# Transposing the first blocks of each memory layer on TensorE instead of by DMA, with a scheduling order of their own

**Chip, cores, metric.** One core of one Trainium2 chip. The metric is the device time of one execution in microseconds (us).

## The reference

Four blocks on a 2048x512 residual stream: memory layer, linear attention, the same memory layer again, linear attention again. Only the memory layer matters here:

```python
def _A_ref(x, mem0, Wq, Wk, Wv, Wo, seg_len):      # x 1x2048x512, 32 heads of 128, seg_len 32, M = 8
    ...
    mem = mem0
    for s in range(n_seg):                          # 64 steps, each needs the memory of the one before
        xs = x[:, s * seg_len:(s + 1) * seg_len, :].copy()
        h = jnp.concatenate([mem, xs], axis=1)      # 8 memory rows + 32 rows of x
        q = jnp.einsum('btd,dhe->bhte', h, Wq)      # k, v likewise
        ...                                         # masked softmax attention, o
        o = jnp.einsum('bhte,hed->btd', o, Wo)
        mem = o[:, :M, :].copy()
        outs.append(o[:, M:, :])
...
x = x + _A_ref(_layernorm(x, axis=-1), A_mem0, A_Wq, A_Wk, A_Wv, A_Wo, A_seg_len)
x = x + _B_ref(_layernorm(x, axis=-1), B_wqkv, B_wo)
x = x + _A_ref(...)                                 # and _B_ref(...) again
```

## The kernel before

The kernel builds a list of nodes (one to some dozens of instructions each) and orders them at build time: each node has a kind and a step, a table `OFFSET` gives the kind's offset, and the priority is step times 13.5 plus offset. An engine then takes the most urgent node that is ready. The waits follow from the data that nodes read and write.

A step projects a block of 32 rows: the 8 memory rows and 24 of the 32 of x. The other 8 rows of four steps are gathered in a "left-over" block, so there are five blocks (and five output projections) in four steps. Queries and keys come out of the projection with the tokens on the partitions and have to be transposed, through an SBUF image, by one of two ways:

```python
def turned(W, key, blk, bkeys, b, dst, dkey, urgent, dma):
    tl = project(W, key, blk, bkeys, b, urgent)                 # 16 matmuls 128x512 into one PSUM bank
    k = img_no[0] % NI if urgent else NI                        # image slot: 3 for the steps, ONE for left-over blocks
    img_no[0] += urgent
    nd = evac(img[:, k, :], lambda: tl.f32()[:, :], 512, ...)   # ScalarE or VectorE
    if dma:
        add("sp", lambda e: e.dma_start_transpose(dst..., img[:, k, :]), 1.25, reads=[("img", k)], ...)
        return nd
    tt = P.tile()
    def tr(pe):                                                 # 16 transposes and 16 weight loads
        for i in range(4):
            for j in range(4):
                r = pe.transpose(tt.bf16()[...], img[:, k, o:o + 32], id_sb[:, :], tile_position=(0, 32 * j))
        return r
    add("pe", tr, ...)
    evac(dst..., lambda: tt.bf16()[:, 0:512], 512, ...)         # a second copy, PSUM to SBUF
    return nd
```

In a step, half of the queries and keys (`b` = 0) goes by DMA and half over TensorE; a left-over block goes by DMA altogether. The loads of the output weights Wo stand in SyncE's order between the transposes:

```python
for i in range(4):                                              # Wo in four quarters of 1 MB
    nd = add("sp", lambda s, hs=hs: s.dma_start(Wo_sb[:, hs, :], wo_view[:, hs, :]), 0.9, writes=[("Wo", i)],
             dsem="dWo%d" % i, after=[late[-2]], ...)           # after the load before the last one
    late.append(nd)                                             # late = [Wq, Wk, Wv, Wo0, Wo1, Wo2, Wo3]
```

The softmax here doesn't subtract the row's maximum and nothing guards it: scores larger than these inputs give would overflow.

## Time and profile before

| | us |
|---|---|
| median of the 3 runs | 1868.53 |
| lowest, highest | 1867.57, 1869.97 |

From the page of the profile (the lines of windows, chain and SyncE that carry the prediction are shown there). First the span, the row of busy times, then two DMA queues with packets, MB and share:

```profile
span 1867.5 us, 95161 instructions
...
PE 1762.9 (94%) x43796; PEld 1201.8 (64%) x43905; DVE 1065.5 (57%) x3267; ACT 1160.3 (62%) x3015; POOL 74.5 (4%) x172
...
q1 hardware_dynamic: 220656, 62.58, 18.1%
...
q8 instruction: 343, 5.62, 1.3%
```

TensorE is busy 94% of the span. q1 carries the transposes.

### The profile page before, as it was taken

To read this page: it belongs to the slowest core of one execution; us is meant where nothing else is said; L and a number is where in the kernel's file an instruction comes from. 1 tells how busy PE (TensorE), PEld (TensorE's weight loads), DVE (VectorE), ACT (ScalarE), POOL (GpSimd) and SP (SyncE) were. 2 spreads that over 40 slices of the span, in tenths; PEclk is the share of its full clock that TensorE was granted. 3 is DMA by queue.
4 is the path that set the end of the run, shared out by engine and by line. 5 is a ranking of instruction groups with operands and counts; after the bars stand their busy time and mean duration, and the time that the engine had idled before them with its cause. 6 is when DMAs were issued, how large, how long until landed. Compare 5 with 4: busy or idle time off the path is not lost.

```text
span 1867.5 us, 95161 instructions
## 1 busy us (share of the span) xinstructions
PE 1762.9 (94%) x43796; PEld 1201.8 (64%) x43905; DVE 1065.5 (57%) x3267; ACT 1160.3 (62%) x3015; POOL 74.5 (4%) x172
## 2 busy tenths in 40 slices
PE   4899999999999999999799999999999999999996
PEld 1566767666666667676456666766667666676662
DVE  1455555656565565655445556556555665565555
ACT  2466666666666666666456666666666666666655
POOL 2000000000000000000000000000000000000000
PEclk8999999999999999999899999999999999999999
DMA  9512121221222121211021222122122221212213
GB/s 336 126 35 42 35 43 37 43 40 37 43 37 43 35 46 37 45 38 40 21 42 35 42 38 48 40 37 45 37 44 42 45 43 38 45 38 54 45 34 124
DMA packets 228256, 96.86 MB, mean 52 GB/s; under 512 B 211624, under 2 KB 222000, under 8 KB 226320
## 3 DMA queue, kind: packets, MB, share of 16 engines
q1 hardware_dynamic: 220656, 62.58, 18.1%
q0 software_dynamic: 5616, 15.60, 2.7%
q10 hardware_dynamic: 1584, 12.58, 1.7%
q8 instruction: 343, 5.62, 1.3%
q14 instruction: 57, 0.47, 0.1%
HBM read 29.89 MB, written 10.49 MB: 22 GB/s over the span
## 4 chain that ended last, share of the span: by engine, by line
PE 85%; DMA 10%; ACT 2%; DVE 2%; issue 1%; SPq 0%; ACTq 0%; DVEq 0%
PE pb L753 39%; PE pb L952 15%; DMA arena_sb<-arena_sb 8%; PE pb L928 4%; PE pb L837 3%; PE pb L775 3%; PE pb L993 3%; PE pb L1088 2%; PE pb L975 2%; PE pb L854 2%; PE pb L892 2%; PE pb L1124 1%; PE pb L868 1%; PE pb L1190 1%; PE pb L867 1%
## 5 line engine op out<-in xcount | busy, mean ns | idle before, releaser
L591 ACT ACTIVATE arena_sb<-pb 128x512 bf16<-128x512 f32 (+6 forms) x1309 | 682.0, 530 | 341.5 <-PE pb L753 272.5
L753 PE MATMUL pb<-Wk_sb,arena_sb 128*32 128x512 bf16 x5120 | 347.7, 383 | 5.5 <-DMA Wk_sb<-in_A_Wk_dram 5.5
L753 PE MATMUL pb<-Wv_sb,arena_sb 128*32 128x512 bf16 x5120 | 352.2, 381 | 0.0
L753 PE MATMUL pb<-Wq_sb,arena_sb 128*32 128x512 bf16 x5120 | 342.2, 383 | 5.4 <-DVE arena_sb L592 4.8
L952 PE MATMUL pb<-Wo_sb,arena_sb 128*32 128x256 bf16 x10368 | 312.3, 275 | 4.9 <-DMA Wo_sb<-in_A_Wo_dram 2.9
L592 DVE CAST arena_sb<-pb 128x128 bf16<-128x128 f32 (+3 forms) x452 | 179.9, 398 | 221.3 <-PE pb L975 110.0
L952 PEld LDWEIGHTS pb<-Wo_sb,arena_sb 128*32 128x32 bf16 x10368 | 274.2, 97 | 20.7 <-DMA Wo_sb<-in_A_Wo_dram 3.4
L913 DVE TENSOR_TENSOR arena_sb<-arena_sb 32x256 bf16<-32x256 bf16 x512 | 212.1, 414 | 50.9 <-ACT arena_sb L909 38.8
L592 DVE COPY arena_sb<-pb 128x512 bf16<-128x512 bf16 (+2 forms) x325 | 121.2, 380 | 191.6 <-PE pb L775 183.9
L753 PEld LDWEIGHTS pb<-Wk_sb,arena_sb 128*32 128x32 bf16 x5120 | 136.9, 97 | 133.6 <-DMA Wk_sb<-in_A_Wk_dram 5.6
L753 PEld LDWEIGHTS pb<-Wq_sb,arena_sb 128*32 128x32 bf16 x5120 | 124.2, 96 | 111.3 <-DVE arena_sb L592 10.6
L753 PEld LDWEIGHTS pb<-Wv_sb,arena_sb 128*32 128x32 bf16 x5120 | 132.5, 97 | 98.1 <-issue 2.8
L591 ACT ACTIVATE outW_sb<-pb 128x128 fp32r<-128x128 f32 x228 | 63.2, 277 | 200.0 <-PE pb L952 198.0
L775 PEld LDWEIGHTS pb<-id_sb,arena_sb 128*32 128x32 bf16 x4096 | 76.4, 96 | 95.0 <-ACT arena_sb L591 47.5
L775 PE MATMUL pb<-id_sb,arena_sb 128*32 128x128 bf16 x4096 | 103.1, 220 | 24.1 <-ACT arena_sb L591 20.2
L928 PE MATMUL pb<-arena_sb 128*128 128x128 bf16 x1024 | 118.7, 217 | 5.5 <-DVE arena_sb L915 5.5
L592 DVE CAST outW_sb<-pb 128x128 fp32r<-128x128 f32 x96 | 28.0, 292 | 161.6 <-ACT outW_sb L591 161.6
L915 DVE TENSOR_TENSOR arena_sb<-arena_sb 32x64 bf16<-32x64 bf16 x512 | 110.8, 216 | 15.7
L844 ACT ACTIVATE arena_sb<-pb 128x256 bf16<-128x256 f32 x252 | 92.1, 383 | 41.1 <-PE pb L837 33.1
L929 PE MATMUL pb<-arena_sb 128*128 128x32 bf16 x1024 | 109.7, 178 | 0.0
L928 PEld LDWEIGHTS pb<-arena_sb 128*128 128x128 bf16 x1024 | 87.8, 96 | 7.2 <-DVE arena_sb L915 5.9
L837 PE MATMUL pb<-arena_sb 128*128 128x32 bf16 x2016 | 89.3, 177 | 2.8 <-DMA arena_sb<-arena_sb 2.5
(109 smaller groups left out, 2270.2 us busy)
## 6 DMA issues: line engine op xcount, KB each, us to landing
arena_sb<-arena_sb SPq DMA_TRANSPOSE x384, 2.5
Wq_sb<-in_A_Wq_dram ACTq DMA_DIRECT2D x1, 4096.0 KB, 13.5
Wk_sb<-in_A_Wk_dram ACTq DMA_DIRECT2D x1, 4096.0 KB, 23.7
Wv_sb<-in_A_Wv_dram ACTq DMA_DIRECT2D x1, 4096.0 KB, 34.4
Wo_sb<-in_A_Wo_dram SPq DMA_DIRECT2D x4, 1024.0 KB, 7.5
xs_scratch<-x_sb POOLq DMA_DIRECT2D x32, 128.0 KB, 2.0
pq_scratch<-arena_sb POOLq DMA_DIRECT2D x32, 128.0 KB, 2.5
x_sb<-xs_scratch POOLq DMA_DIRECT2D x16, 128.0 KB, 2.3
```

The source lines that it names most:

```text
L591: return e.activation(o() if callable(o) else o, i() if callable(i) else i, ACTF.Copy)
L592: return e.tensor_copy(o() if callable(o) else o, i() if callable(i) else i)
L753: r = pe.matmul(tl.f32()[32 * j:32 * j + 32, 0:512], blk[:, c, :], W[:, c, o:o + 512], start=(c == 0), stop=(c == 3), tile_position=(0, 32 ...
L775: r = pe.transpose(tt.bf16()[32 * j:32 * j + 32, 128 * i:128 * i + 128], img[:, k, o:o + 32], id_sb[:, :], tile_position=(0, 32 * j))
L837: r = pe.matmul(tl.f32()[:, o:o + 32], kk[:, hh, :, :].rearrange("p j x -> p (j x)"), qT[:, r2, hh, :, 0:8], start=True, stop=True)
L844: add("act", lambda a: a.activation(Pm[:, k, :, :].rearrange("p a q -> p (a q)"), tl.f32()[:, 0:256], ACTF.Exp, scale=SCALE), c_act(256), ...
L913: add("dve", lambda v, q=q, j=j: v.tensor_tensor(Pbx[q, :, j, 0:32], Px[q, :, :], Rx[q, :, :], ALU.mult), c_dve(256) + 0.075, reads=["Px", ...
L915: add("dve", lambda v, q=q, j=j: v.tensor_tensor(Pbx[q, :, j, 32:40], PLL[q, g2, :, gl], Rx[q, :, 0:8], ALU.mult), c_dve(64) + 0.075, read ...
L928: pe.matmul(o, vimg[:, r2, e], Pbx[:, hh, :, 0:32], start=True, stop=False)
L929: return pe.matmul(o[:, :, 0:8], vleft[:, g2, e], Pbx[:, hh, :, 32:40], start=False, stop=True)
L952: r = pe.matmul(tl.f32()[32 * j:32 * j + 32, 0:256], oT[:, 4 * hh + n, :], Wo_sb[:, 8 * n + hh, 256 * d:256 * d + 256], start=(hh == 0 and ...
L993: r = pe.matmul(tl.f32()[:, 256 * d:256 * d + 256], sel(d), outW[:, u, :], start=first and d == 0, stop=last, skip_group_check=True)
```

## The change

Its intent: in step 0 of each layer and in its first left-over block all transposes go over TensorE, because there the DMA queue is full of weights (layer 1) or the one left-over slot makes the transposes wait for each other (layer 2). The kinds of step 0 get names of their own (suffix F), and the whole table was tuned anew, with a new slack for TensorE's changes of tile size. Cut to its core:

```diff
-MODE_SLACK = 13.03
+MODE_SLACK = 12.37
 OFFSET = {
...          # every offset is new; 10 kinds are added: xlF, qk0F, qk1F, v0F, ... xF
-            P.at(base + s, name + ("F" if s < 0 else "L" if ...))
+            P.at(base + s, name + ("F" if s <= 0 else "L" if ...))
...
-                turned(Wq_sb, "Wq", blk, bk, b, qTl[:, r2, hs, :, :], ("qTl", r2, b), False, True)
-                turned(Wk_sb, "Wk", blk, bk, b, kTl[:, r2, hs, :, :], ("kTl", r2, b), False, True)
+                turned(Wq_sb, "Wq", blk, bk, b, qTl[:, r2, hs, :, :], ("qTl", r2, b), False, step > 0)
+                turned(Wk_sb, "Wk", blk, bk, b, kTl[:, r2, hs, :, :], ("kTl", r2, b), False, step > 0)
...
-                turned(Wq_sb, "Wq", blk, bk, b, qT[:, r2, hs, :, :], ("qT", r2, b), True, QDMA[b])
-                turned(Wk_sb, "Wk", blk, bk, b, kT[:, r2, hs, :, :], ("kT", r2, b), True, KDMA[b])
+                turned(Wq_sb, "Wq", blk, bk, b, qT[:, r2, hs, :, :], ("qT", r2, b), True, QDMA[b] and s > 0)
+                turned(Wk_sb, "Wk", blk, bk, b, kT[:, r2, hs, :, :], ("kT", r2, b), True, KDMA[b] and s > 0)
```

## The prediction

> **What bounds the kernel now.** I first split the span into stages with the table of windows (stretch, its length, then busy us of TensorE, its weight loads, VectorE, ScalarE and GpSimd, the granted TensorE clock, the DMA share, GB/s):
>
> ```profile
> 0.00:57.20 57.20, 26.46 (x407) 11.36 (x411) 12.73 (x35) 15.83 (x41) 13.94 (x61) 0.85 0.95 317
> 57.20:123.00 65.80, 63.58 (x1600) 42.65 (x1604) 32.07 (x104) 39.20 (x106) 1.87 (x3) 0.97 0.26 65
> 123.00:850.00 727.00, 712.37 (x18255) 493.29 (x18288) 430.92 (x1357) 469.25 (x1222) 22.20 (x41) 1.00 0.21 40
> ...
> 931.70:960.00 28.30, 24.31 (x458) 12.24 (x461) 10.87 (x29) 13.57 (x32) 0.54 (x1) 0.88 0.24 40
> 960.00:1019.00 59.00, 57.90 (x1466) 38.60 (x1466) 32.76 (x107) 37.12 (x101) 1.08 (x2) 1.00 0.19 37
> ```
>
> Between the starts of the layers TensorE is busy 98% at full clock: 54 us for four steps. It stands still in the first 57 us (31 of 57, DMA share 0.95) and again around step 0 of the second layer, with the clock at 0.85 and 0.88. So the chain that ended last, there:
>
> ```profile
> 14.38 2.57 PE pb L753 x16
> 16.95 16.63 DMA arena_sb<-arena_sb
> ...
> 35.66 4.95 DMA arena_sb<-arena_sb
> ...
> 41.53 0.53 SPq L766
> 42.07 0.04 issue
> 42.11 6.86 DMA Wo_sb<-in_A_Wo_dram
> 48.97 0.02 issue
> 48.99 8.13 DMA Wo_sb<-in_A_Wo_dram
> 57.12 0.04 issue
> 57.16 2.90 PE pb L952 x64
> ```
>
> L766 is the DMA transpose, L952 the output projection, without which step 1 has no memory. The first transpose took 16.63 us, behind 12.6 MB of Wq, Wk, Wv; and the second quarter of Wo left only at 42.11, though the trace has the last of Wv landed at 36.2 (issued 1.83, 34.4 us to landing). SyncE's own timeline says why:
>
> ```profile
> 24.96 0.39 SPq L629 DMA_DIRECT2D Wo_sb<-in_A_Wo_dram  x1
> 34.28 7.78 SPq L766 DMA_TRANSPOSE arena_sb<-arena_sb  x3
> 42.11 0.58 SPq L629 DMA_DIRECT2D Wo_sb<-in_A_Wo_dram  x1
> ```
>
> SyncE issues in order, and three transposes stood in front. The last of those waited for its image: all left-over transposes share one image slot, so each waits until the one before has landed. The windows show the price: from 40 to 42 us the DMA share is 0.00 with three quarters of Wo still to come.
>
> **What the Trainium skill says.** "VectorE: DVE Perf Modes", section "The three transpose paths", gives 390 ns for a 128x128 bf16 transpose on TensorE and 1309 ns by DMA. Here a DMA transpose moves 128x512, occupies SyncE 1.25 us and lands after a median of 2.5 us (page, DMA issues); 16 TensorE transposes with 32 columns each do the same work in 0.24 to 0.43 us of the chain, so the trace agrees in direction. "TensorE: Matmul & The Clock Gate", section "Part 4: PE-mode transpose", says the result lands in PSUM and needs a copy after; here that copy is the 128x512 bf16 COPY of 0.42 us on VectorE. "DMA: Bandwidth & Descriptors", section "SWDGE vs HWDGE vs iDMA", says a DMA engine round-robins between its queues: agreed, at 22 to 24 us the transposes' queue got 113 packets of 256 B beside 99 of 8 KB. The first page's section "What's actually happening" has the clock at half when TensorE idles; the trace agrees, 0.50 in windows of 3.4 us after the pauses at 20 to 25, 54 to 57 and 946 to 948 us.
>
> **The change, part by part.** It takes four left-over transposes and two of step 0 off the queue in each layer: the orders of both kernels as built show 384 DMA transposes against 372, and 192 more TensorE instructions of 32x128 (12 x 16). Each adds one copy of 0.42 us. The rest is a new table of priorities. Apart from instruction kinds and counts I compared the two orders: TensorE's differ only in the first some 2,000 instructions (to 123 us in the trace of before), around the second layer's start (931.7 to 1019 us), and by three tiny moves in every fourth step. Some small copies move from VectorE to ScalarE. So the steady state stays; I work out the two starts.
>
> Start of layer 1. Six transposes vanish from the congested stretch. SyncE's order is now Wo, Wo, one transpose, Wo, Wo, and the second Wo goes out when Wv lands. When does Wo land?
> - Wv: transposes took about 1 us of DMA time until 36 us; now Wo's first quarter shares instead, at the observed even alternation of packets: about half of its 1024 packets of 1 KB in ten us, 0.5 MB or 1.1 us. So Wv lands at 36.2 as before.
> - 0.5 MB and three quarters of 1.05 MB remain: 3.65 MB at 0.345 MB/us (what Wo moved at from 50 to 54 us) is 10.6; one transpose of 0.85 us between, and 0.9 us for the completion: 36.2 + 12.3 = 48.5 us.
>
> Is TensorE ready by then? After Wv its order has 128 projection matmuls (6.9 us at 54 ns, from 16 in 0.87 us) and some 2.2 us of attention: 9.1 us. Before Wv it has about 7.5 us of work from 25 us on, the first 5 at half clock, plus evacuation waits, so it begins Wv at about 36.5 and is done at 45.6. Wo is the bound: output projection at 48.5 instead of 57.16, 8.7 us. In the new order 32 instructions more lie ahead of it: one projection of 16 (0.87 us) and the 16 x-attention products that took about 1 us after it: 1.8 us. The pause of 3 us before the projection, the half clock after it, and step 1's transposes behind the load of wqkv (chain: 4.30 us at 63.53) all recur. The copies (6 x 0.42 on VectorE) and 6 x 0.25 on TensorE lie in the wait for Wk and Wv, and cost nothing. Sum: 10.5 us.
>
> Start of layer 2. No weights load here; a transpose lands in 2.5 us. From the first projection (931.74) to the selection that makes the next memory (959.45) it takes 27.7 us: 4.0 us idle and two half-clock windows of 3.4 us, each worth 1.7. The cause is the left-over block: its one slot makes transposes leave at 934.4, 941.4, 946.0 and 951.5, so the second half of the memory attention comes at 954.9, 9.4 us after the first. On TensorE the slot comes free after some 0.3 us instead of 2.5. The new order has the first half after 308 instructions: 176 projections 9.5, six transposes 1.5, the rest 1.2, half clock 1.7, evacuation waits 0.8: about 946.4, as before; the second follows at about 949. From there exp, mask, sums, logarithm, reciprocal, product, half a projection, evacuation: 0.4+0.3+0.3+0.3+0.3+0.3+0.9+0.7, some 4 us: the selection at 953, 6.5 earlier. But of the work 41 instructions (2 us) and a few waits are left for later: net 4 us.
>
> Steady state: TensorE idles 14.6 us in 727; earlier copies on the less loaded side may win 1 us over both layers. Sum 10.5 + 4 + 1 = 15.5: 1868.5 - 15.5 = 1853.
>
> **Rivals.**
> (a) Only SyncE's order matters, the DMA time is the bound anyway: then the start wins some 6 us, if Wo's quarters pause between each other as before (6.86 and 8.13 us from issue to landing one after the other, 36.2 + 15 = 51). For it: Wo's third and fourth quarters wait for the first and second. Against: two are in flight at once. Time 1856 to 1858.
> (b) TensorE becomes the bound at the start: transposes there wait for evacuations that ScalarE and VectorE do in order (0.60 and 0.69 us each, now two a group), and six more occupy PSUM banks. If TensorE falls 4 us behind, the output projection comes at 50: a start gain of 9, and in layer 2 the 4 us are gone: 1858. For it: TensorE already waited 7.8 us for ScalarE's images before its own transposes from 12 to 60 us. Against: the long one, 7.1 us, was ScalarE stuck in order behind the DMA transpose, which goes.
> (c) Hidden anyway: layer 2's transposes lie beside 10 us of projections and idle is only 4.0 us, so layer 2 wins nothing or loses the added 1.5 us: 1857 to 1859.
> (d) Better: Wo lands while TensorE is still busy, no pause, clock never halved (0.9 to 1.7 us), wqkv earlier, so step 1 loses its wait as well: 1848.
>
> **Range and chances.** The start may win 7 to 13, layer 2 0 to 7, the steady state -2 to +3. The ends don't coincide, so 1846 to 1860 should hold it 8 times in 10. The 2% line is 1831, a gain of 37 us; all the idle and half-clock loss of both starts that isn't waiting for weights is less. Faster 0.02, within 0.97, slower 0.01.
>
> **What would show it.** Right: the second Wo leaves at about 36 us, the first output projection starts at 47 to 50 after a wait for Wo, four steps still take 54 us, and the second layer's first selection comes about 6 us sooner after its first projection. Wrong: a first output projection after 52, or one that waits for VectorE and not for Wo; a second Wo still behind a transpose; step 0 of layer 2 as long as 27 us; or a difference spread over the steady steps, which would mean that the priorities and not the transposes carry it.

(The section "What's actually happening", which it calls the first page's, is one of "TensorE: Matmul & The Clock Gate".)

## The result, and the profile after

| | median us | lowest to highest | runs |
|---|---|---|---|
| before, same chip | 1868.05 | 1866.47 to 1869.97 | 4 |
| after | 1868.07 | 1865.74 to 1870.37 | 4 |

The ratio is 1.0000, 95% interval 0.9982 to 1.0017 (ratios are the mean time of one kernel's fast runs over that of the other's of the same rounds, so not quite the ratio of the medians). Nothing of the 15.5 us arrived. What did the profile do? The windows of after, cut at the corresponding places (stretch, length, busy us of TensorE, weight loads, VectorE, ScalarE, GpSimd, clock, DMA share, GB/s):

```profile
0.00:51.80 51.80, 26.81 (x531) 13.45 (x531) 15.19 (x42) 17.39 (x45) 13.97 (x61) 0.93 0.97 338
51.80:119.00 67.20, 63.28 (x1587) 41.87 (x1592) 30.52 (x100) 39.17 (x108) 1.87 (x3) 0.98 0.26 62
119.00:845.00 726.00, 710.66 (x18182) 491.00 (x18216) 431.90 (x1325) 472.46 (x1240) 21.71 (x40) 1.00 0.21 40
927.60:960.00 32.40, 31.96 (x779) 18.78 (x783) 15.15 (x46) 21.97 (x53) 0.54 (x1) 0.93 0.11 24
960.00:1014.00 54.00, 49.86 (x1257) 33.04 (x1251) 27.04 (x86) 33.11 (x89) 1.09 (x2) 1.00 0.19 32
```

The first output projection starts 5.3 us earlier (51.87 against 57.16), not 8.7. Step 0 of layer 2 now keeps TensorE busy (31.96 of 32.40 us), but the 54 us after it hold 4.1 us of idle, where before had 1.1 in 59. The chain of after at the start, and SyncE's timeline:

```profile
1.83 34.74 DMA Wv_sb<-in_A_Wv_dram
...
36.59 7.16 DMA Wo_sb<-in_A_Wo_dram
...
43.77 8.05 DMA Wo_sb<-in_A_Wo_dram
...
51.87 3.45 PE pb L963 x64
```

```profile
25.65 11.32 SPq L640 DMA_DIRECT2D Wo_sb<-in_A_Wo_dram  x2
37.67 1.30 SPq L777 DMA_TRANSPOSE arena_sb<-arena_sb  x1
39.03 5.10 SPq L640 DMA_DIRECT2D Wo_sb<-in_A_Wo_dram  x2
```

(Lines of after are 11 above those of before: L963 is the output projection, L777 the DMA transpose, L640 Wo.) The second quarter of Wo leaves when Wv lands, as predicted; but the fourth waits until the second has landed, and each takes 7 to 8 us from issue to landing. The wait table of TensorE (engine, line, what it waited for, us in total, times, longest) has this as the wait:

```profile
PE pb L963 <- DMA Wo_sb<-in_A_Wo_dram: 4.2, 1, 4.2
```

To follow the rest I cut every trace at output projections, which come in the same number in each kernel (162, counted from 0; 81 is the first of layer 2). Mean of three traces of kernels with the timing of before (before itself, its copy c1 and e1, both below) and of two of after:

| stretch | before us | after us | difference | predicted |
|---|---|---|---|---|
| start to projection 10 | 162.1 | 158.8 | -3.4 | -10.5 |
| 10 to 80 (steady, layer 1, and its end) | 746.1 | 748.6 | +2.5 | some -0.5 |
| 80 to 91 (change of layers) | 151.4 | 149.3 | -2.1 | -4 |
| 91 to 151 (steady, layer 2) | 658.5 | 659.2 | +0.7 | some -0.5 |
| 151 to 161 | 99.0 | 101.1 | +2.0 | 0 |
| 161 to end | 48.1 | 48.9 | +0.8 | 0 |

The differences sum to +0.5. So two things failed: the two starts won 5.5 us of the 14.5 that they should, and the steady stretches, which should have stayed, took it back. In the second stretch the three traces of before's timing lie 3.0 us apart (744.7 to 747.7) and the two of after's 2.0, so this table only points; the experiments have to carry it.

### The profile page after: what moved, and what is told of

It reads as the page before. It is cut to its first block, busy times and chain, and to the rows that moved or that the text cites. A ratio compares the mean times of both kernels' runs of the same rounds, so it can differ in the third digit from the quotient of the medians.

```text
span 1865.3 us, 95565 instructions
## 1 busy us (share of the span) xinstructions
PE 1764.4 (95%) x43988; PEld 1205.1 (65%) x44097; DVE 1074.0 (58%) x3227; ACT 1176.7 (63%) x3067; POOL 74.7 (4%) x172
## 4 chain that ended last, share of the span: by engine, by line
PE 83%; DMA 12%; ACT 2%; DVE 2%; issue 1%; ACTq 0%; SPq 0%; DVEq 0%
PE pb L764 38%; PE pb L963 16%; DMA arena_sb<-arena_sb 8%; PE pb L939 3%; PE pb L848 3%; PE pb L786 3%; PE pb L1004 3%; PE pb L1099 2%; PE pb L986 2%; PE pb L903 2%; PE pb L865 2%; DMA Wv_sb<-in_A_Wv_dram 2%; PE pb L1135 1%; PE pb L1201 1%; PE pb L879 1%; PE pb L878 1%
## 5 line engine op out<-in xcount | busy, mean ns | idle before, releaser
L602 ACT ACTIVATE arena_sb<-pb 128x512 bf16<-128x512 f32 (+6 forms) x1360 | 698.7, 523 | 322.2 <-PE pb L764 274.2
L963 PE MATMUL pb<-Wo_sb,arena_sb 128*32 128x256 bf16 x10368 | 312.4, 275 | 6.5 <-DMA Wo_sb<-in_A_Wo_dram 4.2
L603 DVE CAST arena_sb<-pb 128x128 bf16<-128x128 f32 (+3 forms) x445 | 174.4, 392 | 209.3 <-PE pb L986 112.7
L963 PEld LDWEIGHTS pb<-Wo_sb,arena_sb 128*32 128x32 bf16 x10368 | 275.2, 97 | 21.3 <-DMA Wo_sb<-in_A_Wo_dram 4.7
L603 DVE COPY arena_sb<-pb 128x512 bf16<-128x512 bf16 (+2 forms) x293 | 116.7, 407 | 194.2 <-PE pb L786 186.0
L764 PEld LDWEIGHTS pb<-Wv_sb,arena_sb 128*32 128x32 bf16 x5120 | 132.5, 97 | 97.3 <-issue 1.8
L603 DVE CAST outW_sb<-pb 128x128 fp32r<-128x128 f32 x95 | 27.7, 292 | 169.2 <-ACT outW_sb L602 169.1
L786 PE MATMUL pb<-id_sb,arena_sb 128*32 128x128 bf16 x4288 | 107.5, 220 | 17.8 <-ACT arena_sb L602 14.3
```

The costliest lines, as they stand in the source:

```text
L602: return e.activation(o() if callable(o) else o, i() if callable(i) else i, ACTF.Copy)
L603: return e.tensor_copy(o() if callable(o) else o, i() if callable(i) else i)
L764: r = pe.matmul(tl.f32()[32 * j:32 * j + 32, 0:512], blk[:, c, :], W[:, c, o:o + 512], start=(c == 0), stop=(c == 3), tile_position=(0, 32 ...
L786: r = pe.transpose(tt.bf16()[32 * j:32 * j + 32, 128 * i:128 * i + 128], img[:, k, o:o + 32], id_sb[:, :], tile_position=(0, 32 * j))
L963: r = pe.matmul(tl.f32()[32 * j:32 * j + 32, 0:256], oT[:, 4 * hh + n, :], Wo_sb[:, 8 * n + hh, 256 * d:256 * d + 256], start=(hh == 0 and ...
```

## The experiments

Eighteen kernels.

### Which part of the change does it

**a1, the kernel after again.** No edit.

> The changed kernel once more, unaltered, for a second trace and a tighter time. Theory G (the two starts win some 6.5 us, 5.2 and 1.4 in the profile, and the retuned steady steps lose about as much): within 1 us of before, and the second trace again shows four steps taking longer than before's. Theory N (the starts win, and the zero is chance of four runs each, spread 1.5 to 2 us): 2 to 4 us faster than before, and the loss in the steady steps isn't in this trace. Both: first output projection at 51 to 53 us.

Measured: 1871.18 us, ratio 1.0013 (1.0001 to 1.0025). The gain is not hidden by chance; if anything after is slower.

**a2, the flags alone.** The code of after, with the old table and slack (the new F kinds take the offsets of the steady kinds).

```diff
-MODE_SLACK = 12.37
+MODE_SLACK = 13.03
-    "qk0F": (-3.60, -3.55, ...        # every kind back to its value of before
+    "qk0F": (-12.95, -6.45, ...
```

> Transposes of step 0 and of the first left-over block on TensorE, priorities of before (the two added operations take the offset of their evacuation). Theory G: no steady loss, so 3 to 6 us faster than before if the old priorities place the work of step 0 as well as the new. If only the new order makes the transposes pay: within 2 us of before or slower, with the first output projection later than 52 us.

Measured: 1871.41 us, ratio 1.0018 (1.0005 to 1.0030), the first output projection at 52.9 us, and projection 10 at 163.1 us, no earlier than before's 162.1. So without the new order the transposes on TensorE win nothing at the first start, and some 4 us are lost from 10 to 80 (750.3 us) besides.

**a3, the table alone.** The table of after, with the DMA transposes kept.

```diff
-turned(Wq_sb, ..., False, step > 0)          # and the three like it
+turned(Wq_sb, ..., False, True)
```

> The new priorities with every transpose still by DMA. If the transposes carry the start's gain: first output projection at 56 to 58 us as before, time equal or, by theory G, 3 to 6 us slower than before (steady loss without the gain). If the order carries it: first output projection near 52 us.

Measured: 1874.87 us, ratio 1.0042 (1.0030 to 1.0055), with output projection 10 at 169.5 us, 7 later than before; the stretch from 10 to 80 took 747.1 us, as in before, so it is the start that loses. With DMA transposes the new order of the start is a bad one, so the flags and the table belong together.

**a4, new starts, old steady priorities.** The flags, the new offsets of loads and F kinds, and the old offsets and slack for everything else.

```diff
-MODE_SLACK = 12.37
+MODE_SLACK = 13.03
-    "qk0": (-6.35, ...                 # all kinds without F, but the loads, back to before
+    "qk0": (-12.95, ...
```

> The changed kernel with new priorities only in the kinds of the first step, of the first left-over block and of the loads; all steady kinds and the mode slack as before. Theory G: the start's gain without the steady loss, 4 to 7 us faster than before. Theory N: 2 to 4 us faster, the same as the changed kernel within 1.5 us.

Measured: 1865.75 us, ratio 0.9987 (0.9974 to 1.0000). The best of the four, yet only some 2 us. This kernel and a2 are the telling ones: in the steady stretches they have exactly the order and the waits of before on every engine, as a comparison of the orders showed. Yet TensorE's waits from 170 to 810 us add up to 10.0 us in a4 and 12.7 in a2, against 9.0 in before (and 6.6 in its copy c1, below). By time only a2 stands out there: from 10 to 80 it took 750.3 us, a4 746.6, before and c1 747.7 and 744.7.

### Do the starts win anything

**b1, b2, b3: before, after and a4 cut to 512 tokens** (`S = A_x.shape[1]` replaced by `S = 512`; the rows that are not written make the results wrong). Each start is the same; the steady stretches are a quarter as long.

> The kernel before cut to 512 tokens (16 steps in each layer; the result is wrong on purpose, only the first quarter of the rows is written). Both layer starts, the ends and 4 periods of steady steps a layer instead of 16, with the same order of TensorE's first 4,600 instructions and around the second layer's start. Estimate from the traces: 1868 less 24 periods of 54 us is some 570 us. It is the reference for b2 and b3; spread below 1 us.

> The changed kernel cut the same way. Theory S (both starts really win, the long steady stretch loses it in the full kernel): 4 to 7 us less than b1. Rival R (what the starts win is given back within the steps that follow and at the ends, nothing is lost in the steady stretch): within 1.5 us of b1.

> a4 (new kinds at the start, old steady priorities) cut the same way. If the steady priorities don't matter for the starts: within 1 us of b2. If they cost in the steps right after the starts: 1 to 3 us less than b2.

Measured: 545.11, 535.46 and 534.39 us. The short program wins 9.7 us by the change and 10.2 (means) to 10.7 (medians) by the new starts alone. So most of the predicted gain exists, and the long program loses it over its length.

**b4, Wo without the chain.** In after, all of Wo's last three quarters leave when Wv has landed.

```diff
-                 dsem="dWo%d" % i, after=[late[-2]], ...
+                 dsem="dWo%d" % i, after=[late[2]] if i else [late[1]], ...
```

> The changed kernel with Wo's second to fourth quarter all issued when Wv has landed, not each after an earlier quarter (they then also stand ahead of the left-over transpose). The prediction took Wo as bound by bandwidth, landing at 48.5 us. If that is right without the chain of quarters: first output projection at 47 to 49.5 us instead of 51.9, and 2 to 4 us faster than the changed kernel. If bandwidth binds anyway: 51 to 52 us, no change.

Measured: 1868.58 us, ratio 0.9989 (0.9975 to 1.0003), against 1.0000 and 1.0013 for after in its two timings, on other chips; 2 to 4 us of gain over after are not shown. The first output projection came at 49.3 us, close to the predicted 48.5, so the chain of the quarters was the cause of the miss there. But at the fourth one it stood at 91.0 us, after's at 90.9: what is won at the first projection beyond some 5 us is lost in the three steps after it; to what, was not followed.

**c1 to c4: a copy of before; the old starts with the new steady table; before and after at 1024 tokens.**

```diff
 c1: none
 c2: before, with every kind without F and MODE_SLACK from after; loads and first-step kinds as before
 c3: before with S = 1024      c4: after with S = 1024
```

> The kernel before, unchanged, as a kernel of its own. No theory expects a change: ratio 1.0 within 0.002, 1868 to 1870 us. It measures how far two identical programs differ in this comparison, which the later verdicts of 1 to 4 thousandths have to be read against, and gives a second trace of the kernel before. In the first trace the stretch from the 15th to the 70th output projection took 593.5 us, against 595 to 597 in all five kernels whose starts have the transposes on TensorE. Theory S (those starts really leave a slower steady stretch): again 593 to 594 us. Theory N (chance of single traces): anything from 593 to 597.

> The kernel before with its old first-step kinds, loads and DMA transposes, but the new priorities for all steady kinds and the new slack for TensorE's changes of tile size. Theory T (the new steady priorities themselves cost time, as the pair of the kernel after and the one with only the new first kinds suggested, 4.5 us apart): 1871.5 to 1874 us, ratio 1.002 to 1.003. Theory D (the steady priorities are neutral and the loss comes from what the start does to the phase of the rest): 1868 to 1870 us, ratio 1.0 within 0.0015.

> The kernel before cut to 1024 tokens (half the steps of each layer; the results are wrong on purpose, because half of the rows are not written). About 545 + 441 = 986 us, from the 545.1 us at 512 tokens and the 1868.5 us at 2048 (441 us for each 512 tokens). It is the base for the next run.

> The kernel after cut to 1024 tokens (results wrong on purpose). At 512 tokens it was 9.65 us faster than the kernel before, at 2048 tokens 0. Theory L (the starts gain about 12.9 us once and each 512 tokens of steady steps cost 3.2 us): 6.4 us faster, 5 to 8. Theory P (the gain is lost in one place, or is a matter of how the short program happens to lie): 0 to 2, or 9 to 11 us faster.

Measured: c1 1867.56 (ratio 0.9995, 0.9976 to 1.0014), c2 1871.91 (1.0015, 0.9995 to 1.0035), c3 981.38, c4 976.28 us. The change is worth 9.7 us at 512 tokens, 5.3 (means) at 1024 and nothing at 2048: the loss grows with the length. c2 is 2.7 us slower in the mean, but its interval holds 1; the new steady table may cost something, it isn't shown. And c1's 10-to-80 stretch took 744.7 us: another trace in which the DMA starts have the faster steady stretch.

### What the same order does differently

Same order, same waits, more time: what differs must be something that the order doesn't hold. I compared the two traces of one program (before and c1) stall by stall. Many stalls of TensorE recur at the same step in both, so they aren't chance, and in a2 and a4 they recur every 15 output projections (12 steps), at other steps than in before. At about half of them the image slot was late because the issue of a DMA transpose had occupied SyncE for over 1.5 us, mostly 2.0 to 2.5, instead of 1.19. And each of those long issues meets a packet of the queue of kind "instruction" (q8). In four traces (c1, after, d1, e1), counted from the packets in the trace:

| start of the nearest such packet, counted from the issue of the transpose | issues | of them over 1.5 us |
|---|---|---|
| from 1.0 us before it to 0.2 us after it | 322 | 107 |
| 0.2 to 0.6 us after it | 73 | 72 |
| 0.6 to 1.0 us after it | 95 | 45 |
| any other | the remaining 1,034 | 0 |

All 224 long issues lie there, with a third of all issues (in the fifteen full-length traces together 811 of 816).

The other half of the stalls has a second form that the lengths of the issues don't show. A transpose with such a packet 1.0 to 2.0 us after its issue is issued in the usual time, but lands late: in the same four traces, from 120 us on, all 182 of these landed over 3.0 us after their issue (median 4.0, against 2.5 with no packet from 2.5 us before the issue to 3.0 us after it). In eight traces (before, c1, a2, a4, after, d1, d2, e1) TensorE waited 109 times for over 0.25 us from 170 to 810 us: 57 times a long issue stood in the 7 us before the wait, 52 times no long issue but a landing after over 3.0 us, and never neither. At a moment picked at random in that stretch one of the two stands in the 7 us before it 48% of the time.

The Trainium skill has the size: "Advanced Engine Details and Errata", section "ISA Cache", says that a line of the instruction cache is 16 KB and holds 256 instructions. The trace agrees: every packet has 16,384 bytes, and the page of before has 43,905 weight loads of TensorE, which with a matmul each are 87,810 instructions, 343.0 packets of 256; 343 were counted.

This explains the 12 steps. In 12 steps the trace has 4,086 weight loads of TensorE in layer 1 and 4,110 in layer 2, with a matmul each 8,172 and 8,220 instructions: 31.9 and 32.1 packets. So each packet returns to nearly the same place in a step every 12 steps. And it explains how a start can act on everything behind it: the change adds 192 TensorE instructions to layer 1's start (six transposes of 16 loads and 16 matmuls), which moves all later packets against the steps. Here is where the packets lie, as instructions modulo 256 from a fixed place in the order (the 15th output projection in layer 1, the 96th in layer 2):

| | layer 1 | layer 2 |
|---|---|---|
| before, c1, e1 | 205, 204, 204 | 204, 202, 204 |
| after, a1, a2, a4, b4 | 9, 10, 8, 9, 9 | 78, 79, 76, 74, 78 |
| d1 (before + 196) | 8 | 6 |
| d2, d3, d4, e2 (new starts + 62) | 205, 202, 202, 205 | 15, 10, 9, 14 |

Minus 192 is from 204 to 12, minus 384 to 76: what the traces show within 4.

### The test: move the packets and nothing else

The first TensorE work is four tiny transposes at 2.6 us, followed by some 9 us of idle. Extra copies of them there add instructions and change neither order nor waits:

```diff
     def _m0(t, tl=tl):
+        for i in range(98):               # d1: before + 98 (two instructions each); d2, d3, d4, e2: 31; e1: 128
+            c = i % 4
+            t.transpose(tl.bf16()[:, M * c:M * c + M], mem0_sb[0:M, 128 * c:128 * c + 128], id_sb[0:M, 0:M])
         for c in range(4):
```

d1 and e1 are on before, d2 on after, d3 on a4, d4 on a4 with b4's edit to Wo, e2 on after with b4's edit.

> The kernel before with 98 extra 8x8 transposes (196 TensorE instructions) in the idle stretch after its first one at 2.6 us; nothing else differs. This puts the packets that fetch TensorE's program at the place relative to the steps that they have in the kernel after (both kernels' fetches come every 256 instructions; after has some 195 more in its start). Theory F (where the fetches meet the DMA transposes makes the loss in the steady stretch): the slow issues of DMA transposes in layer 1 are at numbers 53, 55, 89, 91, 125 of before's count, as in after, and no more at 29, 31, 65, 67; the stretch from the 10th to the 80th output projection takes 748 to 750 us (before 747.7 and 744.7, after-like kernels 746.6 to 750.3) and the whole 2 to 4 us more, 1870 to 1872.5. Theory R (only chance or something else): slow issues as in before, or moved but no time with them, 1867 to 1869.

> The kernel after with 31 extra 8x8 transposes (62 TensorE instructions) in the same idle stretch, so that its layer 1 has the fetches where the kernel before has them (195 + 62 is 257, one over a fetch of 256). Theory F: slow issues in layer 1 return to the places of before (numbers 23, 25, 59, 61, 95 of after's own count, six less than before's), the stretch from the 10th to the 80th output projection takes 745 to 747.5 us instead of 747.6 to 750.3, and the whole 2 to 3 us less than after: 1865.5 to 1867. Theory R: 1868 to 1870.5, as after.

> The kernel with the new first-step kinds over the old steady priorities, with the same 31 extra transposes. Theory F: 1862 to 1864.5 us (without them 1865.9), ratio to before 0.997 to 0.998, the slow issues at the places of before. Theory R: 1865 to 1867 us.

> As the run before, and Wo's last three quarters issued as soon as Wv has landed (the last no longer waits for the second). It is meant as the fastest kernel. Theory F, with the 1 to 2 us that the earlier Wo was worth in the kernel after: 1861 to 1864 us. If the earlier Wo is worth nothing: as the run before.

> The kernel before with 128 extra 8x8 transposes, 256 TensorE instructions: one whole fetch, so that the places of the fetches against the steps are those of the kernel before again, though more was added than in the run with 98 (1873.4 us mean). Theory F (the place of the fetches): 1866 to 1869.5 us, ratio to before 0.999 to 1.001, slow issues at numbers 29, 31, 65, 67 as in before. Theory A (the added instructions cost the time, by their length or by a later start): 1874 to 1877 us, ratio 1.0035 or more.

> The kernel after with the 31 extra transposes (1863.0 us mean with these alone) and with Wo's last three quarters issued when Wv has landed. If the earlier Wo is worth 3.5 us, the difference between the two kernels with the old steady priorities (1861.2 and 1857.6 us): 1859 to 1860.5 us, and the old steady priorities then are worth the 2 us that remain to the fastest kernel. If it was worth that only with the old priorities: 1862 to 1864 us, as without it.

| | median us | mean | ratio to before (95%) |
|---|---|---|---|
| d1, before with the packets of after's layer 1 | 1875.05 | 1873.4 | 1.0033 (1.0017 to 1.0049) |
| e1, before with one whole packet more | 1870.18 | 1869.9 | 1.0002 (0.9985 to 1.0019) |
| d2, after moved | 1862.88 | 1863.0 | 0.9977 (0.9965 to 0.9990) |
| d3, new starts and old steady table, moved | 1861.76 | 1861.2 | 0.9968 (0.9950 to 0.9986) |
| d4, as d3 with Wo free | 1856.71 | 1857.6 | 0.9949 (0.9936 to 0.9961) |
| e2, d2 with Wo free | 1867.43 | 1867.2 | 0.9986 (0.9971 to 1.0001) |

In absolute times d1 to d4 went beyond theory F's ranges, all in the direction that it expects, e1 ended 0.7 us above its range (its ratio inside), and e2 in neither of its two, on a chip on which before took 1870.1 us in the mean (1867.2 on that of d1 to d4).

d1 and e1 decide it. 196 idle-time instructions slow the kernel before by 6 us; 256 leave it as it was (1.0002). So it is not that instructions were added, but where the packets fall. The long issues moved as expected too: in d1 to numbers 53, 55, 89, 91 and 125, in d2 to 25, 59 and 61 of its own count (23 and 95 were not over 1.5 us), in e1 back to 29, 65 and 67 (not 31). The waits of TensorE from 170 to 810 us, d1 first, then e1 (L778 is its transpose, L806 and L840 are scores, L591 and L592 the evacuations):

```profile
PE pb L778 <- ACT arena_sb L591: 5.0, 6, 1.7
PE pb L806 <- DMA arena_sb<-arena_sb: 3.5, 4, 1.0
PE pb L840 <- DMA arena_sb<-arena_sb: 3.2, 6, 1.1
PE pb L778 <- DVE arena_sb L592: 0.7, 1, 0.7
```

```profile
PE pb L778 <- ACT arena_sb L591: 3.9, 6, 1.2
...
PE pb L806 <- DMA arena_sb<-arena_sb: 1.7, 2, 1.0
PE pb L840 <- DMA arena_sb<-arena_sb: 1.2, 3, 0.6
PE pb L778 <- DVE arena_sb L592: 1.0, 2, 0.6
```

12.4 us against 7.8: the same lines in both, waits that end with a DMA transpose or with an evacuation. Of the 4.6 us between them, 3.8 lie in the waits that end with the transpose itself (6.7 against 2.9). The long issues from 170 to 810 us are as many in d1 as in e1 (22 and 23), so it is their place in a step that differs, and the late landings (41 and 33 over 3.0 us without a long issue). The obvious rival, that TensorE stands because its own program comes late, would show as waits for "issue"; neither table has one. (d1's profiled run was its slowest, 1876.83 us against a mean of 1873.4; e1's was 1868.65 against 1869.9.) Here is one wait behind a long issue, at the same instructions in both kernels. In the timeline of d1 the two transposes of a step take SyncE 3.23 us (1.19 and 1.99; a packet starts at 444.11), ScalarE waits 1.07 us for the image slot, and TensorE 0.81 us for ScalarE:

```profile
442.24 3.23 SPq L769 DMA_TRANSPOSE arena_sb<-arena_sb  x2
...
446.29 1.09 ACT L591 ACTIVATE arena_sb<-pb 128x512 bf16<-128x512 f32 x2 [1.07 <-DMA arena_sb<-arena_sb]
...
446.94 0.41 PE L778 MATMUL pb<-id_sb,arena_sb 128*32 128x128 bf16 x16 [0.81 <-ACT arena_sb L591]
```

In e1 they take 2.64 us, ScalarE waits for no DMA, and TensorE for nothing:

```profile
438.38 2.64 SPq L769 DMA_TRANSPOSE arena_sb<-arena_sb  x2
...
441.27 0.58 ACT L591 ACTIVATE arena_sb<-pb 128x512 bf16<-128x512 f32 x1
...
442.10 0.40 PE L778 MATMUL pb<-id_sb,arena_sb 128*32 128x128 bf16 x16
```

TensorE's waits over all traces, 170 to 810 us (without one group of twelve waits of under 0.2 us in traces that miss some matmul records): 6.6 to 9.0 us in the five with packets near 204 and DMA starts (before, c1, e1, a3, c2), 10.0 to 12.7 in the six with packets near 9 (after, a1, a2, a4, b4, d1), 7.2 to 10.0 in the four moved back (d2, d3, d4, e2).

What doesn't fit: I expected d2 to win its time between projections 10 and 80, at 745 to 747.5 us. It took 748.0 there (d3 746.4, d4 748.1, e2 750.0). By stretches (us):

| stretch | before | after | d1 | d2 | d4 |
|---|---|---|---|---|---|
| to 10 | 162.1 | 158.8 | 165.4 | 159.5 | 156.4 |
| 10 to 80 | 746.1 | 748.6 | 750.2 | 748.0 | 748.1 |
| 80 to 91 | 151.4 | 149.3 | 152.1 | 148.5 | 147.1 |
| 91 to 151 | 658.5 | 659.2 | 659.0 | 658.9 | 657.5 |
| 151 to 161 | 99.0 | 101.1 | 98.7 | 98.3 | 97.3 |
| to the end | 48.1 | 48.9 | 49.7 | 48.1 | 48.1 |

Of the 8.2 us between the traces of d1 and e1, 7.4 lie before projection 80, in layer 1: 4.4 between 10 and 80 (750.2 and 745.8), and 3.0 before 10 (165.4 and 162.4), which I hadn't expected and which is hardly a cost of the added instructions, of which e1 has more (one trace each). But the moved kernels with new starts win mostly in layer 2: 151 to 161 took 98.3, 97.1, 97.3 and 98.9 us in d2, d3, d4 and e2, and 100.5 to 101.2 in all five kernels whose layer-2 packets lie near 76. The same 62 instructions moved those packets too, from 76 to about 12. So the whole gain is there (more than expected in d2), with the larger part where I hadn't looked; no run moved the packets of layer 2 alone.

What the earlier Wo is worth isn't shown: the means of d3 and d4 lie 3.6 us apart on one chip, but their intervals overlap, and from d2 to e2 nothing was won (0.9977 and 0.9986, different chips).

d4 is the fastest kernel found, 0.5% ahead of before, with correct results.

## Why the prediction was wrong, point by point

- **"Sum: 10.5 us", the start of layer 1.** 5.3 us at the first output projection, 3.4 at the tenth. The failed sub-step is the landing of Wo: "3.65 MB at 0.345 MB/us ... 36.2 + 12.3 = 48.5 us" took it as bound by bandwidth, but the fourth quarter waits for the second, 7.16 and 8.05 us one after the other: 51.8. Rival (a) had said 51; its objection "two are in flight at once" was no reason. b4 freed the quarters and got 49.3. The second failed sub-step is silent: that what is won at the first projection is kept. In b4 8 us became 5 within three steps.
- **Order of SyncE and TensorE's readiness.** Right: the second Wo left at 36.59, TensorE waited 4.2 us for Wo and for nothing else at that point.
- **"net 4 us", the start of layer 2.** The mechanism was right: first projection to selection took 21.1 us (927.74 to 948.85), predicted 21.3, before 27.7. (Its last sum, "some 4 us", adds to 3.5.) Yet only 2.1 us of it were left between projections 80 and 91 in the mean of after's two traces (0.6 and 3.7). In the first of them TensorE stood 3.7 of the 54 us after 960 in three waits, at 969.76, 984.48 and 997.49 us, each behind a transpose that had met a packet (an issue of 2.73 us, and landings after 4.0 and 4.1 us). In the four kernels with moved packets the stretch took 147.0 to 148.5 us, 2.9 to 4.4 less than in before. So the 4 us were about right, and what failed here too is that the steps behind a start stay as they were.
- **"So the steady state stays", "may win 1 us".** This is the step that turned a smaller gain into none. It looked at the order and counted the 192 instructions only as time beside other work. The stretches behind the starts took 6.0 us more (2.5, 0.7, 2.0 and 0.8); with the packets moved (d2) the same four took 1.6 us more than before's. By d1 and e1, the place of TensorE's instruction packets alone is worth 6 us in the kernel before, and with it changed after becomes 0.23% faster than before (d2). The prediction named "a difference spread over the steady steps" as a sign that the priorities carry it; the difference was there, and a2, with the old priorities, had it too (750.3 us from 10 to 80). So that reading of the sign was wrong as well.
- **Size without the packets.** The short program wins 9.7 us; d2, whose layer 1 has the packets of before, 4.2 of 1867.2. Either way 15.5 was too much.
- **Open.** How much the new steady table costs: a1 and a4, 4.5 us apart on one chip with intervals that don't overlap, point to a cost where the packets lie as in after, but after's first timing (1.0000) doesn't; c2 (+2.7 us in the mean) and d2 against d3 (1.8) are within the noise. How the gain of the moved kernels divides between the layers. Whether the earlier Wo pays. Where the gain of the first projection goes in the steps after it. And why some meetings cost and others don't: the loss was shown by the place of the packets, at two places in layer 1 and three in layer 2, and not by the DMA engine that they used.

## What to carry to other kernels

When two kernels have the same order in a stretch and different times there, look at what the order doesn't hold: a program of tens of thousands of instructions is itself DMA traffic, and here its packets delayed the transposes that they met. Before judging a change of a few tenths of a per cent, add or remove instructions in an idle stretch, up to one packet of 256, as a control, and scan that shift as one more parameter to tune. And a gain at the start counts only where the steps behind it can keep it: follow it over the first ten steps, not to the first one.

## What the Trainium skill lacked or had wrong

- "Advanced Engine Details and Errata", section "ISA Cache", has the 16 KB and 256 instructions, which the traces confirm (343 to 345 packets of 16,384 bytes). The loading itself stands in "Runtime: NRT & Kernel Launch", section "Instruction fetch mechanics", which has it run over a DMA queue of its own (q8 here). What both lack is what it does to other transfers: 224 of 224 DMA transposes whose issue took over 1.5 us (1.19 usually, up to 2.7) met such a packet, in all traces 811 of 816.
- "DMA: Bandwidth & Descriptors", section "DMA Transpose (X-bar)", doesn't say that a transpose can hold its issuing engine for 1.5 to 2.5 us instead of 1.19 when such a packet starts 0.2 to 0.6 us after the issue (72 of 73), nor that it lands later when the packet starts 1.0 to 2.0 us after it (4.0 us instead of 2.5; 182 of 182 over 3.0).
- No page says that instructions added in one place can change the time of steps far behind it: 196 TensorE instructions in an idle stretch cost the kernel before 6.2 us (d1), 256 cost nothing (e1, ratio 1.0002).
